# When the parts of the first layer's weight forms are made, and how the first maxima of W1 are taken

## The chip, the cores and the metric

The kernel runs on one core of a Trainium2 chip. A time is the device time of one execution in microseconds. It was measured three times: 1002.93, 1004.01 and 1005.3 us. The engines are TensorE (PE, with its weight loads as PEld), VectorE (DVE), ScalarE (ACT), GpSimd (POOL) and SyncE (SP), which issues the DMAs.

## What is computed

```python
def _attn_ref(q, k, v, tau):                      # q, k, v: (1, 6016, 256)
    qn = q / (np.linalg.norm(q, axis=1, keepdims=True) + 1e-06)
    kn = k / (np.linalg.norm(k, axis=1, keepdims=True) + 1e-06)
    s = kn.transpose(0, 2, 1) @ qn / tau
    a = np.exp(s - s.max(-1, keepdims=True))
    a /= a.sum(-1, keepdims=True) + 1e-09
    return v @ a                                  # (1, 6016, 256)

x = _attn_ref(q, k, v, tau).reshape(6016, 256)
h = x @ w_in1;  x = (h * np.cos(h)) @ w_out1      # 256 -> 2048 -> 256
h = x @ w_in2;  x = (h / (1 + np.exp(-h))) @ w_out2
```

The attention matrix a is only 256x256 (over channels), so the kernel folds it into the first layer: W1 = a @ w_in1.

## The kernel before, in words

Every matmul operand is kept in two parts, hi (the value rounded to the short form that the matmul takes) and lo (what is left), and a product takes three passes: hi by hi, lo by hi, hi by lo. The tokens are cut into 12 blocks, 11 of 512 and one of 384. The 2048 inner columns are cut into 8 pairs m of 256.

The program has these stages. The attention's scores and norms are made from q and k, about the first 50 us. Then W1 is folded in four pieces j (tile `wa0` to `wa3`, 512 columns each) while blocks 0 to 2 already run through the first layer in 24 units (`units`: a block b and a pair m). The rest of the first layer, and the second layer, run in slots after that. There a block's product is done in 7 products of quarter size instead of 8, on sums and differences of quarters: the forms. They need forms of the weights too: for each piece k of W1 `form_w1(k)` makes the four sums and differences, and `split_w1(k)` their hi and lo parts (`wf`).

There is no scheduler. `tc.manual_schedule()` leaves each engine's queue in the order in which the code emits the instructions, and an engine that waits holds up all that stands behind it. The order is set by tables: `BEFORE` lists the steps ahead of the first unit, `FORMING` says after which unit which steps of the forms stand, A0 for `form_w1(0)`, B0 for `split_w1(0)`, and V for a step of splitting and forming block 3's v (`v_steps`).

One pass of the loop over units, for unit i:
- PE: h of unit i (`emit_h`, 12 matmuls, L823), then, behind the other engines' steps in the code but alone on its own queue, o of unit i-2 (`emit_o1`, 12 matmuls, L851).
- ACT and DVE: the hi (L834) and lo (L838) of unit i-1, then the Sin of unit i (L1177) on ACT and the product with h (L1179) on DVE.
- At i = 4, 8, 12, 15 and 22 a small matmul of maxima (L442 or L477) and a comparison on DVE (L449 and L450, or L481 and L482) check that the arguments of Sin stay in range, and their room in PSUM is the one into which the next h goes.
- The steps of `FORMING[i]`. `form_w1` has two sums on DVE (L1031, `w1base`) and four sums or differences on POOL (L1039, `w1form`); `split_w1` has one copy on ACT (L1045, the hi) and two subtractions on POOL (L1047, the lo).
- The steps of x2, the input of layer 2 of a finished block (`begin_x2`: L917 to L919 on ACT, L936 to L945 on DVE or POOL).

A piece's base and form tiles have two buffers each (`raw` and `wv`), which v's form and the second layer's weights use too.

Ahead of the first unit, from `BEFORE`: `T0 T1` transposes, `rs` adds 1e-9 to the sums of the softmax and takes the reciprocal (L690, L691), `x0` takes v's maxima for block 0 (L430), `f00 f01` fold the two halves of piece 0 (PE L729, ACT L737), `l00 l01` make their lo (DVE L741), and `w00 w01` take the largest magnitude of piece 0 for each half of the channels (DVE L460), for the small matmul (L442) that stands between the h of unit 0 and of unit 1.

Of the kernel before, what the change touches and what calls it, by code (L numbers as in the profile page):

```python
# [9 lines left out]
F32 = mybir.dt.float32  # L10
F32R = mybir.dt.float32r
BF16 = mybir.dt.bfloat16
# [4 lines left out]
ALU = mybir.AluOpType  # L17
AX = mybir.AxisListType
PSUM = bass.MemoryType.PSUM

P = 128
C = 256
CH = C // P
# [35 lines left out]
THEN = ['', '', 'jO s0', '']  # L59
SIDE = [7, 11, 15, 20]  # L60
JOINED = 22
BEFORE = 'v0 sO T0 T1 bW kW x0 rs f00 lv l00 f01 l01 w00 w01 tb'
TURNS = 16
OPENED = 13
FORMING = {13: 'A0', 14: 'B0 A1', 15: 'B1 A2', 16: 'B2 A3', 17: 'B3 V', 18: 'V', 19: 'V'}
DOUBLED = (17, 22)
EARLY = {
# [21 lines left out]
@with_exitstack  # L89
def attention_then_two_ffns(ctx: ExitStack, tc: tile.TileContext, qk, vT, tau, w_in1, w_out1, w_in2, w_out2, outT):  # L90

    nc = tc.nc

    dp = ctx.enter_context(tc.tile_pool(name="dp", bufs=1, space=bass.MemoryType.DRAM))
    fp = ctx.enter_context(tc.tile_pool(name="fp", bufs=1))  # L100
    within = fp.tile([1, 1], I32, name="within")
    ctx.enter_context(tc.manual_schedule())
    kept = [[dp.tile([P, 2, 2, PIECE], F32, name=f"{s}{i}_kept") for i in range(4)] for s in ("wa", "wo1_")]
    with ExitStack() as rooms:
        direct(rooms, tc, qk, vT, tau, w_in1, w_out1, w_in2, w_out2, outT, dp, kept, within)
    inside = nc.values_load(within[0:1, 0:1], min_val=0, max_val=1)
    with tc.If(inside == 0):
        with ExitStack() as rooms:
            general(rooms, tc, vT, w_in2, w_out2, outT, kept)
# [117 lines left out]
def direct(ctx, tc, qk, vT, tau, w_in1, w_out1, w_in2, w_out2, outT, dp, kept, within):  # L227
    nc = tc.nc

    wp = ctx.enter_context(tc.tile_pool(name="wp", bufs=1))  # L230
# [12 lines left out]
    wa = [wp.tile(QUAD, F32R, tag="quad", name=f"wa{i}", bufs=8) for i in range(4)]  # L243
# [12 lines left out]
    largest = wp.tile([P, 4, CH], BF16, name="largest")  # L256
# [153 lines left out]
    def load_v(b):  # L410
        t0, n = BLOCKS[b]
        raw = io.tile([P, CH, TB], F32, tag="vraw", name=f"vraw{b}", bufs=1)
        nc.sync.dma_start(out=raw[:, :, :n], in_=vT.rearrange("(a p) n -> p a n", p=P)[:, :, t0 : t0 + n])
        return raw

    def span_of(b, raw, a=None):
# [9 lines left out]
            apply_absolute_value=True,  # L426
        )

    def span_of_first(b, raw):
        nc.vector.tensor_reduce(  # L430
            out=firsts[:, :, b],
            in_=raw.rearrange("p a (j n) -> p a j n", n=P),
            axis=AX.X,
            op=ALU.max,
            apply_absolute_value=True,
        )
# [22 lines left out]
    def span_of_weights(j, a):  # L459
        nc.vector.tensor_reduce(  # L460
            out=largest[:, j, a : a + 1],
            in_=fold_to(j, a, 0).bitcast(F32),
            axis=AX.XY,
            op=ALU.max,
            apply_absolute_value=True,
        )
# [19 lines left out]
    def split_v(b, raw):  # L486
        n = BLOCKS[b][1]
        hi, lo = xparts[1, b] = [x_tile(s, b) for s in ("hi", "lo")]
        nc.scalar.activation(halves(hi[:, :, :n]), turns(raw[:, :, :n]), AF.Copy)

        def low(eng=nc.vector):
            eng.tensor_tensor(
                out=halves(lo[:, :, :n]), in0=turns(raw[:, :, :n]), in1=halves(hi[:, :, :n]).bitcast(F32), op=ALU.subtract
            )

        return low
# [24 lines left out]
    rs = pp.tile([P, CH], F32, name="rs")  # L521
# [11 lines left out]
    calls = {  # L533
        "V": lambda: raw_v.update({0: load_v(0)}),
        "s0": lambda: low_v.update({0: split_v(0, raw_v[0])}),
        "v0": lambda: low_v.pop(0)(nc.gpsimd),
        "x0": lambda: span_of_first(0, raw_v.pop(0)),
        "lv": lambda: raw_v.update({1: load_v(1)}),
        "x1": lambda: span_of_first(1, raw_v[1]),
        "s1": lambda: low_v.update({1: split_v(1, raw_v[1])}),  # L540
        "v1": lambda: low_v.pop(1)(),
# [15 lines left out]
    def steps_of(names):  # L557
        for name in names.split():
            calls[name]()
# [107 lines left out]
    for a in range(CH):  # L667
        nc.vector.scalar_tensor_tensor(
            out=E[:, a], in0=S[a], scalar=r[:, 1, a : a + 1], in1=rq, op0=ALU.mult, op1=ALU.mult
# [54 lines left out]
    def fold_half(m):  # L724
        fold_room(0, m)
        for a in range(CH):
            pws[0, a] = pws[0, a][:, : TB // 2]
            for d in range(CH):
                nc.tensor.matmul(  # L729
                    pws[0, a],  # L730
                    ET[:, d, a * P : (a + 1) * P],
                    w1[:, d, m * TB // 2 : (m + 1) * TB // 2],
                    start=(d == 0),
                    stop=(d == CH - 1),
                )
        for a in range(CH):
            nc.scalar.activation(fold_to(0, a, 0)[:, m], pws[0, a], AF.Copy, scale=rs[:, a : a + 1])  # L737

    def fold_low_half(m):
        for a in range(CH):  # L740
            nc.vector.scalar_tensor_tensor(  # L741
                out=fold_to(0, a, 1)[:, m],
                in0=pws[0, a],
                scalar=rs[:, a : a + 1],
                in1=fold_to(0, a, 0)[:, m].bitcast(F32),
                op0=ALU.mult,
                op1=ALU.subtract,
            )

    def fold_whole(j):  # L750
        fold_room(j, 0)
        for a in range(CH):
            fold(j, a)

    def fold_highs(j):
        for a in range(CH):
            fold_high(j, a)

    def fold_to(j, a, i):
        return wa[j][:, i].rearrange("p m (a f) -> p a m f", a=CH)[:, a]  # L760

    def fold_low(j, a):
        nc.vector.scalar_tensor_tensor(
            out=fold_to(j, a, 1),
            in0=pws[j, a].rearrange("p (m f) -> p m f", m=2),
            scalar=rs[:, a : a + 1],
            in1=fold_to(j, a, 0).bitcast(F32),
            op0=ALU.mult,
            op1=ALU.subtract,
        )  # L770

    for j in range(NF // 4):
        calls[f"f{j}"] = lambda j=j: fold_whole(j)
        calls[f"e{j}"] = lambda j=j: fold_highs(j)
        for a in range(CH):
            calls[f"f0{a}"] = lambda a=a: fold_half(a)
            calls[f"l{j}{a}"] = (lambda j=j, a=a: fold_low(j, a)) if j else (lambda a=a: fold_low_half(a))
            calls[f"w{j}{a}"] = lambda j=j, a=a: span_of_weights(j, a)
    steps_of(BEFORE)
    early.close()  # L780

# [275 lines left out]
    def w2_slot(name, m):  # L1057
        w = w2[name][m]
        return lambda i, k: w[:, i, k - NS + w.shape[2]]
# [126 lines left out]
    for i, u in enumerate(units):  # L1186
        b, m = u
# [46 lines left out]
        if i == TURNS - 1:  # L1234
            vraw = load_v(FIRST + 1)
        for what in FORMING.get(i, "").split():
            if what == "V":
# [299 lines left out]
    for j in range(len(slots) + LAG2):  # L1537
        u, p, q, o = [slots[j - d] if 0 <= j - d < len(slots) else None for d in (0, 1, 2, LAG2)]
        if j < J:
# [5 lines left out]
        u, p, q, o = [  # L1545
            None if v is not None and v[:2] == (2, PLAIN) else v for v in (u, p, q, o)
        ]
        first_p, first_q, first_o = [v if v is not None and v[0] == 1 else None for v in (p, q, o)]
        p, q, o = [None if w_ is not None else v for v, w_ in ((p, first_p), (q, first_q), (o, first_o))]
# [5 lines left out]
        if p is not None:  # L1555
            k = (j - 1) % 2
            w = w2_slot("wi2", p[2])
            x = xparts[p[:2]]
            y, x0, z = ys[k][:, 1], xz[k][:, 1], xz[k][:, 0]
# [124 lines left out]
```

## Time and profile before

| | |
|---|---|
| times of three runs | 1002.93, 1004.01, 1005.3 us |
| the profiled execution | 1004.25 us |
| its span, first to last instruction | 1002.5 us |
| mean granted clock of TensorE | 0.998 |
| PE busy | 983.4 us (98%), 7080 matmuls |
| DVE, ACT, POOL busy | 819.1, 785.1, 400.4 us |
| chain that ended last | PE 87%, POOL 3% |

The chain is followed back from the last instruction; the matmuls' ends are modelled, so a gap between two matmuls is read best from when they start. Busy shares are means over the whole program; a wait counts in the stage in which it stands.

### The profile page before, as it was taken

To read this page: it belongs to the slowest core of one execution; us is meant where nothing else is said; L and a number is where in the kernel's file an instruction comes from. 1 tells how busy PE (TensorE), PEld (TensorE's weight loads), DVE (VectorE), ACT (ScalarE), POOL (GpSimd) and SP (SyncE) were. 2 spreads that over 40 slices of the span, in tenths; PEclk is the share of its full clock that TensorE was granted. 3 is DMA by queue.
4 is the path that set the end of the run, shared out by engine and by line. 5 is a ranking of instruction groups with operands and counts; after the bars stand their busy time and mean duration, and the time that the engine had idled before them with its cause. 6 is when DMAs were issued, how large, how long until landed. Compare 5 with 4: busy or idle time off the path is not lost.

```text
span 1002.5 us, 18729 instructions
## 1 busy us (share of the span) xinstructions
PE 983.4 (98%) x7080; PEld 929.8 (93%) x7080; DVE 819.1 (82%) x1287; ACT 785.1 (78%) x1442; POOL 400.4 (40%) x378
## 2 busy tenths in 40 slices
PE   9999998999999999999999999999999999999998
PEld 7878876899999999999999999999999999999997
DVE  6787775978787888787875789999999999999972
ACT  6776645688888888888876887887888888888863
POOL 4453358538777687787473111111111111111100
PEclk9999999999999999999999999999999999999999
DMA  8931021914334334334479731121121121121101
GB/s 334 383 110 63 1 93 72 350 74 160 137 126 142 133 144 142 152 131 153 147 256 383 312 147 43 55 95 49 47 96 49 48 96 55 45 93 39 36 18 41
DMA packets 35012, 126.59 MB, mean 126 GB/s; under 512 B 3170, under 2 KB 4450, under 8 KB 30178
## 3 DMA queue, kind: packets, MB, share of 16 engines
q1 hardware_dynamic: 34770, 125.12, 33.7%
q8 instruction: 57, 0.93, 0.4%
q14 instruction: 41, 0.34, 0.1%
q10 hardware_dynamic: 144, 0.20, 0.1%
HBM read 73.01 MB, written 52.30 MB: 125 GB/s over the span
## 4 chain that ended last, share of the span: by engine, by line
PE 87%; POOL 3%; ACT 1%; DVE 1%; issue 1%; ACTq 0%; POOLq 0%; DVEq 0%
PE o L1065 20%; PE xz L1065 20%; PE o L1421 16%; PE ys L1065 15%; PE o L851 6%; PE h L823 3%; POOL w1form L1039 2%; PE o L1105 2%; PE pw L711 1%; POOL wf L1047 1%; PE xz L1094 1%; PE ys L1094 1%; PE ys L1376 1%; PE xz L1376 1%; PE bound L823 1%
## 5 line engine op out<-in xcount | busy, mean ns | idle before, releaser
L881 DVE TENSOR_TENSOR lo<-t,hi 128x768 fp32r<-128x768 f32 (+1 forms) x176 | 194.8, 1116 | 29.2 <-ACT hi L873 29.1
L868 POOL TENSOR_TENSOR t<-t 128x256 f32<-128x256 f32 x88 | 64.4, 732 | 356.8 <-DVE t L865 312.9
L873 ACT ACTIVATE hi<-t 128x768 fp32r<-128x768 f32 (+1 forms) x176 | 168.6, 958 | 26.8 <-PE o L1065 25.9
L1421 PE MATMUL o<-hi,wo 128*128 128x512 f32 x512 | 142.0, 380 | 0.0
L1065 PE MATMUL o<-hi,wo 128*128 128x256 f32 x770 | 134.7, 275 | 0.0
L1065 PEld LDWEIGHTS o<-hi,wo 128*128 128x128 f32 x770 | 117.1, 192 | 0.0
L1065 PE MATMUL o<-lo,wo 128*128 128x256 f32 x385 | 105.9, 275 | 0.0
L1421 PEld LDWEIGHTS o<-hi,wo 128*128 128x128 f32 x512 | 87.4, 190 | 6.8
L1475 DVE TENSOR_TENSOR xz<-xz,t 128x512 f32<-128x512 f32 x64 | 44.8, 700 | 42.0 <-ACT t L1469 41.1
L1421 PE MATMUL o<-lo,wo 128*128 128x512 f32 x256 | 76.1, 380 | 0.0
L1065 PE MATMUL ys<-xhi,wf 128*128 128x256 f32 x384 | 74.2, 275 | 0.3 <-ACT u L1512 0.3
L1065 PEld LDWEIGHTS ys<-xhi,wf 128*128 128x128 f32 x384 | 67.7, 190 | 7.3 <-ACT u L1512 0.5
L1065 PEld LDWEIGHTS o<-lo,wo 128*128 128x128 f32 x385 | 73.9, 192 | 0.0
L1065 PE MATMUL xz<-xhi,wa 128*128 128x256 f32 x384 | 71.8, 276 | 0.0
L1580 ACT ACTIVATE ys<-xz 128x256 f32<-128x256 f32 x88 | 32.4, 368 | 45.8 <-PE xz L1065 44.9
L851 PE MATMUL o<-hi,wo 128*128 128x512 f32 (+1 forms) x256 | 64.2, 373 | 3.6 <-ACT hi L834 3.6
L1065 PEld LDWEIGHTS xz<-xhi,wa 128*128 128x128 f32 x384 | 62.8, 191 | 3.4
L1065 PE MATMUL xz<-x2hi,wf 128*128 128x256 f32 x352 | 65.8, 275 | 0.0
L1065 PE MATMUL xz<-x2hi,wa 128*128 128x256 f32 x352 | 65.8, 275 | 0.0
L860 DVE TENSOR_TENSOR t<-t 128x512 f32<-128x512 f32 x88 | 60.3, 685 | 0.1
L1610 ACT ACTIVATE t<-t 128x512 f32<-128x512 f32 x88 | 55.6, 632 | 2.2 <-DVE t L1115 2.1
L1466 ACT ACTIVATE ys<-xz 128x256 f32<-128x256 f32 x64 | 23.6, 368 | 40.9 <-PE xz L1065 39.8
(277 smaller groups left out, 3156.4 us busy)
## 6 DMA issues: line engine op xcount, KB each, us to landing
qk<-qk_dram SPq DMA_DIRECT2D x22, 512.0 KB, 7.7
x2hi<-xshi SPq DMA_DIRECT2D x11, 896.0 KB, 4.9
x2lo<-xslo SPq DMA_DIRECT2D x11, 896.0 KB, 6.9
wi_dram<-stage SPq DMA_DIRECT2D x8, 1024.0 KB, 3.8
wo_dram<-stage SPq DMA_DIRECT2D x8, 1024.0 KB, 4.2
vraw<-vT_dram SPq DMA_DIRECT2D x11, 512.0 KB, 4.1
outT_dram<-q SPq DMA_DIRECT2D x22, 256.0 KB, 2.0
xshi<-t SPq DMA_DIRECT2D x10, 512.0 KB, 5.4
```

The lines of the kernel that those rows point to most:

```text
L823: nc.tensor.matmul(hp[:, s, :n], wa_at(i, a, 2 * m + s), columns(x[k][:, a, :n]), start=((i, k) == passes[0] and a == 0), stop=((i, k) == ...
L851: nc.tensor.matmul(o[:, e, :n], wo1_at(i, f)[:, e * P : (e + 1) * P], columns(parts[k][:, s, :n]), start=(f == 0 and (i, k) == PASSES[0]), ...
L860: eng.tensor_tensor(out=t[:, 4:6, :c], in0=t[:, 0:1, :c].to_broadcast([P, 2, c]), in1=t[:, 1:3, :c], op=ALU.subtract)
L868: eng.tensor_tensor(out=t[:, 7, :c], in0=t[:, 3, :c], in1=t[:, 6, :c], op=ALU.subtract)
L873: nc.scalar.activation(hi[:, sl, :c], t[:, 1:][:, sl, :c], AF.Copy)
L881: nc.vector.tensor_tensor(out=lo[:, sl, :c], in0=t[:, 1:][:, sl, :c], in1=hi[:, sl, :c].bitcast(F32), op=ALU.subtract)
L1065: nc.tensor.matmul(out, w(p, ka), columns(x[r][:, kb - 1]), start=(start and i == 0), stop=(stop and i == 2), skip_group_check=True,)
L1421: nc.tensor.matmul(o[:, e], wo1_at(i, f)[:, e * P : (e + 1) * P], columns(parts[k][:, s]), start=(f == 0 and (i, k) == PASSES[0]), stop=(f ...
L1466: nc.scalar.activation(y2, x2, AF.Copy)
L1475: nc.vector.tensor_tensor(out=xz[k], in0=xz[k], in1=sines[:, 1], op=ALU.mult)
L1580: nc.scalar.activation(y2, x2, AF.Copy)
L1610: nc.scalar.activation(t[:, 0:2], t[:, 0:2], AF.Silu)
```

## The change

`FORMING` is written anew, the order of `BEFORE` is changed, and the first piece's maxima are taken in another way.

```diff
-BEFORE = 'v0 sO T0 T1 bW kW x0 rs f00 lv l00 f01 l01 w00 w01 tb'
+BEFORE = 'v0 sO T0 T1 bW kW rs f00 x0 lv l00 w00 f01 l01 w01 tb'
-FORMING = {13: 'A0', 14: 'B0 A1', 15: 'B1 A2', 16: 'B2 A3', 17: 'B3 V', 18: 'V', 19: 'V'}
+FORMING = {13: 'A0', 14: 'A1', 15: 'B0', 16: 'B1', 17: 'V', 18: 'V A2', 19: 'V', 20: 'B2 A3', 22: 'B3'}
+    half = wp.tile([P, CH], BF16, name="half")
+
+    def span_of_half(m):
+        to = half if m else largest[:, 0]
+        nc.vector.tensor_reduce(
+            out=to,
+            in_=wa[0][:, 0, m].rearrange("p (a f) -> p a f", a=CH).bitcast(F32),
+            axis=AX.X,
+            op=ALU.max,
+            apply_absolute_value=True,
+        )
+        if m:
+            nc.vector.tensor_tensor(out=largest[:, 0], in0=largest[:, 0], in1=half, op=ALU.max)
...
-            calls[f"w{j}{a}"] = lambda j=j, a=a: span_of_weights(j, a)
+            calls[f"w{j}{a}"] = (lambda j=j, a=a: span_of_weights(j, a)) if j else (lambda a=a: span_of_half(a))
```

For piece 0 `w00` and `w01` now stand for the first and the second half of its columns, each reduced for both halves of the channels in one instruction, and the two results are joined by a maximum. Lines behind the added function are 14 higher in the new file.

ACT at units 14 to 17, before (`wf0` to `wf3` are the hi of the forms, `hi` that of a unit, `t` a Sin, `xhi` the hi of v, `y` and `spare` are x2's):

```order
L489 ACTIVATE xhi2_1031<-vraw2_953 128x1024
L1045 ACTIVATE wf0_965<-w1form0_995 128x2x512
L834 ACTIVATE hi0_497<-t0_495 128x1024
L1177 ACTIVATE t1_496<-h1_7_1059,half_pi_98,smalls_102 128x1024
L1045 ACTIVATE wf1_966<-w1form1_1040 128x2x512
L834 ACTIVATE hi1_498<-t1_496 128x1024
L1177 ACTIVATE t0_495<-bound15_1080,half_pi_98,smalls_102 128x1024
L1045 ACTIVATE wf2_967<-w1form2_1093 128x2x512
```

The same place on ACT in the changed kernel:

```order
L503 ACTIVATE xhi2_1033<-vraw2_955 128x1024
L848 ACTIVATE hi0_499<-t0_497 128x1024
L1191 ACTIVATE t1_498<-h1_7_1058,half_pi_98,smalls_102 128x1024
L1059 ACTIVATE wf0_967<-w1form0_997 128x2x512
L848 ACTIVATE hi1_500<-t1_498 128x1024
L1191 ACTIVATE t0_497<-bound15_1079,half_pi_98,smalls_102 128x1024
L1059 ACTIVATE wf1_968<-w1form1_1039 128x2x512
```

The hi of unit 14 now stands ahead of `wf0`, and each `wf` of the first two pieces one unit later; `wf2` and `wf3` stand further down, behind the Sins of units 20 and 22.

POOL behind the forms of piece 0, before (`w1form` the forms, `wf` their lo):

```order
L1047 TENSOR_TENSOR wf0_965<-w1form0_995,wf0_965 128x512 x2
L1039 TENSOR_TENSOR w1form1_1040<-w1base1_1039 128x2x128 x2
L1039 TENSOR_TENSOR w1form1_1040<-w1form1_1040,w1base1_1039 128x2x128
L1039 TENSOR_TENSOR w1form1_1040<-w1base1_1039,w1form1_1040 128x2x128
L1047 TENSOR_TENSOR wf1_966<-w1form1_1040,wf1_966 128x512 x2
L1039 TENSOR_TENSOR w1form2_1093<-w1base2_1092 128x2x128 x2
L1039 TENSOR_TENSOR w1form2_1093<-w1form2_1093,w1base2_1092 128x2x128
L1039 TENSOR_TENSOR w1form2_1093<-w1base2_1092,w1form2_1093 128x2x128
```

The same place on POOL in the changed kernel (`vform` and `xlo` are the forms and the lo of v's block 3):

```order
L1053 TENSOR_TENSOR w1form1_1039<-w1base1_1038 128x2x128 x2
L1053 TENSOR_TENSOR w1form1_1039<-w1form1_1039,w1base1_1038 128x2x128
L1053 TENSOR_TENSOR w1form1_1039<-w1base1_1038,w1form1_1039 128x2x128
L1061 TENSOR_TENSOR wf0_967<-w1form0_997,wf0_967 128x512 x2
L1061 TENSOR_TENSOR wf1_968<-w1form1_1039,wf1_968 128x512 x2
L1012 TENSOR_TENSOR vform3_1155<-vraw3_1086 128x256 x2
L1012 TENSOR_TENSOR vform3_1155<-vraw3_1086,vform3_1155 128x256 x2
L1012 TENSOR_TENSOR xlo3_1153<-vraw3_1086,xhi3_1152 128x768
L1053 TENSOR_TENSOR w1form2_1196<-w1base2_1195 128x2x128 x2
```

The forms of piece 1 stand directly behind those of piece 0, both pieces' lo behind them, and v's forms and raw lo ahead of the forms of piece 2.

DVE ahead of the first unit, before (`rs` are the softmax's sums, `firsts` v's maxima, `largest` W1's):

```order
L680 COPY ET_125<-pt1_452 128x2x128
L430 TENSOR_REDUCE firsts_103<-vraw0_401 128x2x4
L690 TENSOR_SCALAR rs_127<-rs_127 128x2
L691 RECIPROCAL rs_127<-rs_127 128x2
L741 SCALAR_TENSOR_TENSOR wa0_89<-pw00_468,rs_127,wa0_89 128x256 x2
L741 SCALAR_TENSOR_TENSOR wa0_89<-pw01_479,rs_127,wa0_89 128x256 x2
L460 TENSOR_REDUCE largest_99<-wa0_89 128x1 x2
L449 TENSOR_REDUCE o1_0_514<-o1_0_514 128x1
```

The same place on DVE in the changed kernel:

```order
L694 COPY ET_126<-pt1_453 128x2x128
L704 TENSOR_SCALAR rs_128<-rs_128 128x2
L705 RECIPROCAL rs_128<-rs_128 128x2
L444 TENSOR_REDUCE firsts_103<-vraw0_402 128x2x4
L755 SCALAR_TENSOR_TENSOR wa0_89<-pw00_468,rs_128,wa0_89 128x256 x2
L433 TENSOR_REDUCE largest_99<-wa0_89 128x2
L755 SCALAR_TENSOR_TENSOR wa0_89<-pw01_481,rs_128,wa0_89 128x256 x2
L433 TENSOR_REDUCE half_104<-wa0_89 128x2
L441 TENSOR_TENSOR largest_99<-largest_99,half_104 128x2
L463 TENSOR_REDUCE o1_0_516<-o1_0_516 128x1
```

The reciprocal stands ahead of v's maxima, one reduction of W1 stands between the two lo steps, and one reduction and the maximum behind them.

## Rows read from the trace of the kernel before

**Rows 1.** Stages: us, then each engine's busy us, granted clock, DMA share, GB/s.

```profile
120.00:200.00 80.00, 72.58 (x326) 60.38 (x325) 59.04 (x59) 42.82 (x48) 50.25 (x37) 0.98 0.41 159
420.00:1002.00 582.00, 576.97 (x4750) 569.20 (x4749) 490.86 (x799) 465.34 (x938) 145.04 (x166) 1.00 0.29 107
```

**Rows 2.** Timeline of PE, 148 to 177 us: start, us, line, instruction, idle before.

```profile
148.37 1.99 PE L823 MATMUL bound<-xhi,wa 128*128 128x512 f32 x4 [2.42 <-DVE smalls L482]
...
155.31 1.03 PE L823 MATMUL h<-xhi,wa 128*128 128x512 f32 x4
...
160.49 1.03 PE L823 MATMUL h<-xhi,wa 128*128 128x512 f32 x4
...
164.55 1.13 PE L851 MATMUL o<-hi,wo 128*128 128x512 f32 x4 [1.31 <-ACT hi L834]
...
168.06 1.03 PE L823 MATMUL h<-xhi,wa 128*128 128x512 f32 x4
...
173.12 1.13 PE L851 MATMUL o<-hi,wo 128*128 128x512 f32 x4 [2.31 <-ACT hi L834]
...
176.91 1.03 PE L823 MATMUL h<-xhi,wa 128*128 128x512 f32 x4
```

**Rows 3.** One microsecond of the same view as rows 1, from 149 us.

```profile
149.00:150.00 1.00, 1.00 (x4) 0.82 (x3) 1.00 (x2) 0.00 (x0) 1.00 (x3) 0.50 0.97 410
```

**Rows 4.** Timeline of ACT, units 14 to 16.

```profile
145.42 1.04 ACT L834 ACTIVATE hi<-t 128x1024 fp32r<-128x1024 f32 x1
146.37 1.19 ACT L1177 ACTIVATE t<-h,half_pi,smalls 128x1024 f32<-128x1024 f32 x1
...
161.46 1.06 ACT L1045 ACTIVATE wf<-w1form 128x1024 fp32r<-128x1024 f32 x1 [5.50 <-POOL w1form L1039]
...
163.43 1.06 ACT L834 ACTIVATE hi<-t 128x1024 fp32r<-128x1024 f32 x1
```

**Rows 5.** Timeline of DVE, units 13 to 15.

```profile
137.70 1.28 DVE L1031 TENSOR_TENSOR w1base<-wa 128x512 f32<-128x512 f32 x2
138.90 1.22 DVE L838 TENSOR_TENSOR lo<-t,hi 128x1024 fp32r<-128x1024 f32 x1
140.03 1.22 DVE L1179 TENSOR_TENSOR t<-h,t 128x1024 f32<-128x1024 f32 x1
...
142.65 2.32 DVE L1031 TENSOR_TENSOR w1base<-wa 128x512 f32<-128x512 f32 x2
146.49 1.45 DVE L838 TENSOR_TENSOR lo<-t,hi 128x1024 fp32r<-128x1024 f32 x1 [1.52 <-ACT hi L834]
...
148.06 0.16 DVE L482 TENSOR_SCALAR smalls<-bound 128x1 f32<-128x1 f32 x1
```

**Rows 6.** POOL busy in L1039 (four pieces' forms), 136 to 186 us.

```profile
136.00:186.00 50.00, 16.89 (x16) 0.97 0.37 147
```

**Rows 7.** The same of L1047 (four pieces' lo).

```profile
136.00:186.00 50.00, 11.99 (x8) 0.97 0.37 147
```

**Rows 8.** The same of L998 (block 3's v: forms, raw lo, formed lo).

```profile
136.00:186.00 50.00, 11.97 (x7) 0.97 0.37 147
```

**Rows 9.** Groups by line of POOL, 136 to 186 us: busy, mean ns, idle before.

```profile
L998 POOL TENSOR_TENSOR xlo<-vform,xhi 128x512 fp32r<-128x512 f32 x2 | 4.5, 2266 | 0.0
```

**Rows 10.** Timeline of POOL: block 4's v.

```profile
192.68 2.37 POOL L998 TENSOR_TENSOR vform<-vraw 128x256 f32<-128x256 f32 x2 [7.46 <-DMA vraw<-vT_dram]
```

**Rows 11.** Timeline ahead of and at the first units.

```profile
51.98 1.21 DVE L430 TENSOR_REDUCE firsts<-vraw 128x8 bf16<-128x1024 f32 x1
...
53.59 0.84 ACT L737 ACTIVATE wa<-pw,rs 128x256 fp32r<-128x256 f32 x2 [0.47 <-DVE rs L691]
...
56.76 1.27 DVE L460 TENSOR_REDUCE largest<-wa 128x1 bf16<-128x512 f32 x2
...
58.09 0.18 PE L442 MATMUL o<-firsts,largest 128*128 128x4 bf16 x1 [0.41 <-DVE largest L460]
...
70.02 3.70 PE L711 MATMUL pw<-w,ET 128*128 128x512 f32 x8 [0.45 <-POOL w L320]
```

## The prediction

> **What bounds the kernel now.** The matmul engine's share comes first, by stages: from 420 us on it is busy 576.97 of 582 us, and what is missing there is the end of the program; from 120 to 200 us it is busy only 72.58 of 80, at a mean granted clock of 0.98 [rows 1]. That is the stage of units 13 to 23, in which the parts of W1's forms are made, and the change is made there. The reader is to see that time can come from hardly anywhere else.
>
> Second, the matmul timeline of that stage, read by the starts of h, the first product of a unit. A unit is 24 matmuls (12 of h, 12 of o) and takes 5.18 us where nothing waits, as from 155.31 to 160.49; that is 0.216 each. The h of unit 16 starts at 148.37 after 2.42 us idle. From there to the next h pass 6.94 us, 1.76 too many; from unit 18's h (160.49) to unit 19's (168.06) 7.57, 2.39 too many; from there to unit 20's (176.91) 8.85, 3.67 too many [rows 2]. Together 10.24 us.
>
> No wait stands beside the 1.76. They are the clock: 0.50, the level of 1.2 GHz, in the microsecond from 149 [rows 3], and four matmuls took 1.99 us. The engine had stood for 2.42 us; after 2.31 us before 173.12 four of them took 1.13 [rows 2], so that time the clock stayed. The length of the wait alone does not tell the two apart.
>
> Third, why h and o wait. On ACT the high part of the forms (wf, L1045) stands ahead of the unit's own high part (hi, L834). Before the third wf ACT sat idle 5.50 us until POOL had the form; hi came behind it, at 163.43, and at 145.42 in unit 14 [rows 4]. DVE's lo of unit 14 begins at 146.49 after 1.52 idle, and L482, which releases the h of unit 16, at 148.06 [rows 5]. So POOL and ACT in turn pace four units: forms of 16.89 / 4 = 4.2 us a piece [rows 6] and lo parts of 11.99 / 4 = 3.0 [rows 7].
>
> **The change, part by part.** No instruction of PE or SP moves; DVE gets two more.
>
> *Unit 14 to 16.* The wf of piece 0 goes behind the Sin of unit 15, so hi of unit 14 waits only for DVE's product: 140.03 + 1.22 = 141.25 instead of 145.42. Its lo is now held by DVE itself, whose row of work ends with the base of piece 1 at 142.65 + 2.32 = 144.97 [rows 5]. From lo's start to the h of unit 16 it took 148.37 - 146.49 = 1.88, so h starts at 146.85: 1.52 won, 0.9 of wait left. I take the clock to stay up, since that wait is shorter than the 1.31 before 164.55, behind which the engine went on at 1.13 for four [rows 2]: 1.76 won. Bounds: 0, where the drop comes all the same, and 1.76.
>
> *Units 16 to 19.* Are the 2.39 and 3.67 us gone, once hi is free of wf? I follow each new place of a wait, at POOL's mean durations. POOL has the first forms at 145.42 - 1.06 = 144.4 [rows 4]. The h of unit 15 ends 2.9 before the o that ended at 148.37 - 2.42, at 143.1, and Sin takes 1.19; ACT asks for wf 0 at 144.3 and waits 0.1. The forms of piece 1 last from 145.0 to 149.2 on POOL; wf 1 comes behind the Sin of unit 16, at 150.6, and does not wait. What lies between wf and hi in that unit (three copies) let hi start 163.43 - 161.46 = 1.97 behind wf; so hi at 152.6, lo 1.45 behind its 1.06: 155.2. The o of unit 16 is due at 146.85 + 5.18 + 5.18 + 2.59 = 159.8: over 4 us to spare. POOL goes on with both lo parts to 155.2, then the forms and raw lo of v (11.97 less 4.5 for the formed lo [rows 8, 9]) to 162.7, the forms of piece 2 (its base ends near 164.5) to 168.7, the formed lo to 173.2, lo 2 to 176.2 and the forms of piece 3 to 180.4. ACT asks for v's form near 166, for piece 2 at 171.4 and for piece 3 at 181.8 (Sin of units 19, 20, 22): 3, 2.7 and 1.4 us after POOL has them. Where POOL is 2 us slower, hi of unit 22 is late by 0.6, against some 3 us of room in o. So all of 2.39 + 3.67 = 6.06 is won; the bound below is 2.39, where the longer stall comes back once.
>
> DVE's bases of pieces 2 and 3 move to units 18 and 20, behind those units' products. With 1.3 to 2.3 us [rows 5] they go into units of 5.18 in which product and lo take 2.4 to 2.9; unit 18 also holds an x2 part as large as lo's three quarters, and overruns by some 0.5, covered by the 3 us that its lo has until o. If that cover were gone the 0.5 would show in o.
>
> *Bases beside POOL.* A base of two instructions takes 1.28 us before POOL begins (137.70) and 2.32 beside its forms; lo takes 1.22 and, beside POOL's lo parts, 1.45 [rows 5]. Behind the change POOL hardly rests from 139 to 186, so the long durations stand in the sums above. The Trainium skill (SBUF — State Buffer, Who interferes with whom) is harsher: of a DVE instruction with two inputs in SBUF and a GpSimd one that reads there, whichever starts second is blocked until the first has finished. By that rule lo of unit 14 could stand through a whole form, about 1.06 us at the mean, where the trace lengthens it by 0.23; the sum would be smaller by some 0.8, and I go by the row.
>
> *The front.* DVE took v's maxima (1.21 us at 51.98) ahead of the reciprocal for which ACT's fold waited until 53.59; now the reciprocal is first. That alone moves nothing, because the second half's fold waits for matmuls. What counts stands behind it: two reductions at 56.76, 1.27 us together, release the matmul at 58.09. Now the first half is reduced while DVE was idle, only one reduction is left behind the second half, and a maximum over 128x2 follows. No row shows that one; L482, as small, takes 0.16 [rows 5]. Half of 1.27 less 0.16 and its issue is 0.4; between 0 and the 0.6 that h of unit 1 waits in all I take 0.35. It travels through Sin, v's split and the decode to the matmuls that waited for POOL until 70.02 [rows 11]. v's second load waits for the maxima that now end 0.5 later; I price that at nothing, or the 0.35 back.
>
> Sum: 1.52 + 1.76 + 6.06 + 0.35 = 9.69. The profiled execution took 1004.25 us (its span 1002.5), 0.24 above the median of the runs shown; 1004.25 - 9.69 = 994.6 us. What is won by 200 us reaches the end, since the matmul engine has no gap behind it to give it back in [rows 1].
>
> **The rivals.**
> *Unit 16 keeps its wait and the clock drops (0.14).* For it: the h of unit 16 still waits for DVE, and POOL now runs through. If base and lo take 1.5 us longer, nothing is won there. Against it: the long durations are in the sum already. Left are 6.06 + 0.35: 997.8 us. The Trainium skill (TensorE: Matmul & The Clock Gate, HAM oscillation) has waits take the array to half its clock and the work behind them run cold; here one wait of three did. By that rule with the short wait 1.76 come back: 996.4 us.
>
> *The wait moves on (0.07).* Pieces 2 and 3 now share POOL with v's forms, and the margin at unit 22 is 1.4 us. If ACT meets POOL late at unit 20 or 22 as it did at 16 and 17, 2.39 to 3.67 come back: 997.0 to 998.3 us.
>
> *Nothing comes of it (0.04).* POOL's row of work falls behind throughout and both waits return, with the clock: 6.06 + 1.76 back, 1002.4 us or above.
>
> *Slower (0.03).* POOL begins the next block's v form near 186, when the matmul engine is 2 to 3 us further on than before; there POOL had 7.46 us idle ahead of it [rows 10]. ACT's copy of such a form stands ahead of its own work in each of seven blocks. If POOL is late for that copy from then on, each block loses the lateness; from 9.69 / 7 = 1.4 us a block it is slower than before, and at 2.5 us it is 994.6 + 17.5 = 1012 us. Against it: the copy comes two slots behind the form.
>
> **How the numbers follow.** The forecast has 0.72, the rivals 0.14, 0.07, 0.04 and 0.03. Under 0.2%, 2 us, a measurement of this kernel can't be told from no change. Faster by more: 0.72 + 0.14 + 0.07 = 0.93; same 0.04; slower 0.03. Low end: the waits of 10.24 and 0.6 at the front all won, 993.4, and 0.9 for the scatter of the runs: 992.5. High end: the first two rivals, 998.3.
>
> **What would show it.** Right: from 120 to 200 us the matmul engine's idle time falls from 7.4 us to near 1, and the clock stays 1.00; wf waits under 0.5 us on ACT; the o of units 16 and 17 waits for nothing; the h of unit 16 waits about 0.9 us, behind a base on DVE; the second matmul on the maxima comes at about 57.7 and the fold of piece 1 at 69.7. Wrong: an ACT wait above 3 us on wf of pieces 2 or 3 or on v's form, or a clock of 0.50 anywhere behind 60 us.

## The result, and the profile after

The changed kernel took 994.42 us (median of six runs, 993.16 to 996.48), the kernel before 1004.22 (six runs, 1002.93 to 1005.3). The ratio is 0.9905, with an interval of 0.9892 to 0.9917: 9.8 us less, where the prediction's sum had 9.69. The profiled execution took 994.43 us, its span 992.6 (before 1002.5), its mean granted clock was 0.999 (0.998). One execution of the second experiment below took 1456.11 us at a mean granted clock of 0.654, a slower state, and is left out of that experiment's median.

The stage of units 13 to 23 is where it went. The same windows as in [rows 1], the last one to the end of the shorter span, and the microsecond of [rows 3]:

```profile
120.00:200.00 80.00, 79.85 (x394) 68.90 (x393) 65.53 (x71) 51.11 (x63) 53.17 (x38) 1.00 0.47 178
420.00:992.00 572.00, 566.94 (x4683) 559.82 (x4681) 482.67 (x785) 455.86 (x920) 138.22 (x160) 1.00 0.29 106
149.00:150.00 1.00, 1.00 (x6) 0.89 (x5) 0.56 (x1) 0.98 (x1) 1.00 (x1) 1.00 0.99 418
```

From 120 to 200 us the matmul engine idles 0.15 us instead of 7.42, and the clock stays at 1.00. From 200 to 420 us it is busy 220.00 of 220 us in both traces, and from 420 us to the end it idles 5.06 us, before 5.03: nothing is given back.

The timeline of the matmul engine in that stage (start, us, line, instruction, idle before), against [rows 2]; line numbers are 14 higher than before:

```profile
146.09 1.10 PE L837 MATMUL bound<-xhi,wa 128*128 128x512 f32 x4 [0.15 <-DVE smalls L496]
...
151.35 1.03 PE L837 MATMUL h<-xhi,wa 128*128 128x512 f32 x4
...
156.53 1.03 PE L837 MATMUL h<-xhi,wa 128*128 128x512 f32 x4
...
161.71 1.03 PE L837 MATMUL h<-xhi,wa 128*128 128x512 f32 x4
...
164.30 1.03 PE L865 MATMUL o<-hi,wo 128*128 128x512 f32 x4
165.16 0.59 PE L865 MATMUL o<-lo,wo 128*128 128x512 f32 x2
...
166.89 1.03 PE L837 MATMUL h<-xhi,wa 128*128 128x512 f32 x4
```

These are the h of units 16 to 20, and between the last two the o of unit 17. The h of unit 16 starts 2.28 us earlier than before (146.09 against 148.37); the fold of piece 1 starts at 70.02 in both traces, so the starts can be compared as they stand. From there to unit 17's h pass 5.26 us where it was 6.94, 1.68 won. From unit 17's h to unit 20's pass 15.54, three units at the full pace; before it was 176.91 - 155.31 = 21.60, so 6.06 are won. Sum: 10.02, and unit 20 starts 176.91 - 166.89 = 10.02 earlier. No wait stands beside the o of unit 17, at 164.30 and 165.16; before, it waited 2.31 us and then 0.82.

ACT in units 13 to 20, against [rows 4]:

```profile
141.37 1.06 ACT L848 ACTIVATE hi<-t 128x1024 fp32r<-128x1024 f32 x1 [0.59 <-DVE widest L483]
...
146.29 1.07 ACT L1059 ACTIVATE wf<-w1form 128x1024 fp32r<-128x1024 f32 x1 [1.79 <-POOL w1form L1053]
...
150.18 1.07 ACT L1059 ACTIVATE wf<-w1form 128x1024 fp32r<-128x1024 f32 x1
...
165.66 1.04 ACT L1030 ACTIVATE xhi<-vform 128x1024 fp32r<-128x1024 f32 x1
...
170.84 1.04 ACT L1059 ACTIVATE wf<-w1form 128x1024 fp32r<-128x1024 f32 x1
```

The hi of unit 14 starts at 141.37 instead of 145.42. Only the first wf waits for POOL, 1.79 us, and behind it nothing is late: hi of unit 15 has until its o at 153.94.

DVE in units 13 to 15 against [rows 5], and POOL's form of piece 0 that ran beside it:

```profile
142.70 1.29 DVE L1045 TENSOR_TENSOR w1base<-wa 128x512 f32<-128x512 f32 x2
143.89 1.78 DVE L852 TENSOR_TENSOR lo<-t,hi 128x1024 fp32r<-128x1024 f32 x1
...
145.79 0.16 DVE L496 TENSOR_SCALAR smalls<-bound 128x1 f32<-128x1 f32 x1
```

```profile
141.50 3.09 POOL L1053 TENSOR_TENSOR w1form<-w1form,w1base 128x256 f32<-128x256 f32 x1
```

The base of piece 1 took 1.29 us, not 2.32. POOL was the slower for it: this form of 128x256 took 3.09, where the sixteen form instructions, in their three groups, had medians of 0.90, 1.05 and 1.59. It does not always go this way: in the last experiment, which is the same kernel, the base took 2.33 and this form 1.85.

The front, against [rows 11]:

```profile
50.91 3.62 PE L743 MATMUL pw<-w,ET 128*128 128x256 f32 x16
...
57.97 0.20 PE L456 MATMUL o<-firsts,largest 128*128 128x4 bf16 x2 [0.85 <-DVE largest L441]
58.04 1.11 PE L837 MATMUL h<-xhi,wa 128*128 128x512 f32 x4
...
70.02 2.41 PE L725 MATMUL pw<-w,ET 128*128 128x512 f32 x5 [0.57 <-POOL w L320]
```

```profile
50.28 2.42 POOL L506 TENSOR_TENSOR xlo<-vraw,xhi 128x1024 fp32r<-128x1024 f32 x1
...
51.46 1.27 DVE L704 TENSOR_SCALAR rs<-rs 128x2 f32<-128x2 f32 x1
...
52.76 0.17 DVE L705 RECIPROCAL rs<-rs 128x2 f32<-128x2 f32 x1
...
56.23 0.68 DVE L433 TENSOR_REDUCE half<-wa 128x2 bf16<-128x512 f32 x1
...
56.87 3.62 POOL L303 TENSOR_SCALAR w<-w 128x1024 f32<-128x1024 f32 x1
56.95 0.97 DVE L441 TENSOR_TENSOR largest<-largest,half 128x2 bf16<-128x2 bf16 x1
```

The times of the program's start scatter from run to run: the first matmul of the fold (L743) began at 51.44 before, at 50.91 here, and between 49.59 and 50.91 in the experiments. So the front is read as intervals from that matmul. The h of unit 1 came 6.69 us behind it before and comes 7.13 behind it now; the fold of piece 1 18.58 before, 19.11 now. The front lost 0.4 to 0.5 us, where 0.35 was predicted to be won. The maximum over 128x2 took 0.97, not 0.16, and the addition of 1e-9, now first on DVE, 1.27.

### The profile page after: what moved, and what is told of

Read it like the earlier page. It is cut to its first block, busy times and chain, and to the rows that moved or that the text cites. A ratio compares the mean times of both kernels' runs of the same rounds, so it can differ in the third digit from the quotient of the medians.

```text
span 992.6 us, 18733 instructions
## 1 busy us (share of the span) xinstructions
PE 980.5 (99%) x7080; PEld 928.6 (94%) x7080; DVE 820.7 (83%) x1288; ACT 785.3 (79%) x1442; POOL 402.9 (41%) x378
## 4 chain that ended last, share of the span: by engine, by line
PE 90%; DVE 2%; ACT 1%; issue 1%; POOL 0%; ACTq 0%; DVEq 0%
PE o L1079 20%; PE xz L1079 20%; PE o L1435 16%; PE ys L1079 15%; PE o L865 7%; PE h L837 4%; PE o L1119 2%; PE pw L725 1%; PE bound L837 1%; PE xz L1108 1%; PE ys L1108 1%; PE ys L1390 1%; PE xz L1390 1%; DVE xlo L506 0%; DVE lo L852 0%
```

## The experiments

My theory behind the result: all of the gain is the order of the forms' parts, and the front costs half a microsecond, because two small DVE instructions meet POOL there. Rivals: the front has a part in the gain; a single step of `FORMING` would have done; the small maximum is slow by its shape.

**The forms' order alone** (on the kernel before):

```diff
-FORMING = {13: 'A0', 14: 'B0 A1', 15: 'B1 A2', 16: 'B2 A3', 17: 'B3 V', 18: 'V', 19: 'V'}
+FORMING = {13: 'A0', 14: 'A1', 15: 'B0', 16: 'B1', 17: 'V', 18: 'V A2', 19: 'V', 20: 'B2 A3', 22: 'B3'}
```

> The new FORMING alone, the front as before. Theory: the whole gain is FORMING's (10.0 us between the o of unit 14 and the h of unit 20) and the new front costs about 0.45 us, because two 2-element DVE instructions stand beside a running POOL instruction (the addition to rs 1.27 us, the maximum 0.97). Then this kernel takes 993.9 us, ratio 0.9897, and its fold of piece 1 starts 18.6 us after the first fold matmul, as before (19.1 in the changed kernel). Rival: the new front wins the 0.35 us of the prediction and its lateness in the one profile is chance; then this kernel takes 994.8 us and shows the 18.6 us all the same, while the front alone is faster.

It took 994.2 us (ratio 0.9901, 0.9884 to 0.9917): the whole gain, as far as times can tell. Whether the front adds or takes half a microsecond is read from the traces. The h of unit 1 came 6.69 behind the first fold matmul, as before. The timeline of its matmuls:

```profile
50.91 3.62 PE L729 MATMUL pw<-w,ET 128*128 128x256 f32 x16
...
57.60 1.11 PE L823 MATMUL h<-xhi,wa 128*128 128x512 f32 x4
...
146.06 1.10 PE L823 MATMUL bound<-xhi,wa 128*128 128x512 f32 x4 [0.65 <-DVE smalls L482]
```

**The front alone** (on the kernel before):

```diff
-BEFORE = 'v0 sO T0 T1 bW kW x0 rs f00 lv l00 f01 l01 w00 w01 tb'
+BEFORE = 'v0 sO T0 T1 bW kW rs f00 x0 lv l00 w00 f01 l01 w01 tb'
+    (and span_of_half for piece 0's maxima)
```

> The new BEFORE and the maxima by halves alone, FORMING as before. Theory: 0.45 us slower than before, 1004.7 us; the h of unit 1 starts 7.1 us after the first fold matmul (before 6.69) and the fold of piece 1 19.1 us after it (before 18.58); all waits of units 16 to 19 as before. Rival: 0.35 us faster, 1003.9 us, the h of unit 1 at 6.3 us and the fold at 18.2.

It took 1004.85 us (median of nine executions), ratio 1.0011 (1.0001 to 1.0021): no gain, and a trace of a loss. The interval from the first fold matmul to h of unit 1 was 7.13, as in the changed kernel. In the middle it showed something else:

```profile
147.85 1.10 PE L837 MATMUL bound<-xhi,wa 128*128 128x512 f32 x4 [2.55 <-DVE smalls L496]
...
164.08 2.08 PE L865 MATMUL o<-hi,wo 128*128 128x512 f32 x4 [3.04 <-ACT hi L848]
...
169.36 1.42 PE L837 MATMUL h<-xhi,wa 128*128 128x512 f32 x4
...
172.83 1.13 PE L865 MATMUL o<-hi,wo 128*128 128x512 f32 x4 [0.33 <-ACT hi L848]
...
176.44 1.03 PE L837 MATMUL h<-xhi,wa 128*128 128x512 f32 x4
```

```profile
168.00:170.00 2.00, 2.00 (x6) 1.56 (x5) 1.22 (x2) 0.99 (x2) 0.90 (x2) 0.50 0.00 0
```

Behind the wait of 2.55 us four matmuls took 1.10, the full pace. Behind the next one, 3.04, they took 2.08; the granted clock was 0.50 there. So the clock fell once, as in the kernel before, but at another place, and it was still at 0.50 from 168 to 170 us. The stage lost no more by it: the waits of the o of unit 17 were 0.33 and 0.64 us instead of 2.31 and 0.82, and from the wait at unit 16 to the h of unit 20 there were 2.55 + (176.44 - 147.85) - 4 x 5.18 = 10.42 us too many, where the kernel before has 10.24. Here the slow stretch was in part time that would have been waited anyway.

**The copy and the lo parts of piece 0 back to unit 14** (on the changed kernel):

```diff
-FORMING = {13: 'A0', 14: 'A1', 15: 'B0', 16: 'B1', ...
+FORMING = {13: 'A0', 14: 'B0 A1', 16: 'B1', ...
```

> The changed kernel with the parts of piece 0 put back to unit 14 (FORMING 14: 'B0 A1'), all else as changed. Theory: hi of unit 14 waits again behind wf of piece 0, the h of unit 16 starts about 2.3 us later (148.4 instead of 146.1), and the clock falls behind that wait as before: 994.4 + 2.3 + 1.7 = 998.4 us; the o of units 16 and 17 wait for nothing. Rival: the clock fell for another reason than this wait and stays at 1.00: 996.7 us.

It took 996.88 us (0.9935, 0.9919 to 0.9952). Its h of unit 16 and 17, and the microsecond behind the wait:

```profile
148.43 1.10 PE L837 MATMUL bound<-xhi,wa 128*128 128x512 f32 x4 [2.54 <-DVE smalls L496]
...
153.68 1.03 PE L837 MATMUL h<-xhi,wa 128*128 128x512 f32 x4
```

```profile
149.00:150.00 1.00, 1.00 (x6) 0.88 (x5) 0.41 (x1) 0.49 (x1) 1.00 (x3) 1.00 1.01 426
```

The wait of the h is back, through the same chain as in [rows 4, 5]: ACT stood 3.79 us for POOL's form, hi began at 145.48, DVE's lo at 146.55. The h starts 2.34 us later than in the changed kernel (148.43 against 146.09), the span is 2.4 us longer (995.0 against 992.6) and the median 996.88 - 994.42 = 2.46. The clock stayed in this trace: 5.25 us from h to h. My expectation that the clock falls whenever this wait comes was wrong, and three of the four executions, 996.5 to 996.91 us, are as the rival said (996.7). The fourth took 998.72 us at a mean granted clock of 0.997, near the theory's 998.4; it was not profiled, so where its clock fell is not known.

**Piece 2 and 3 back to units 16 to 18** (on the changed kernel):

```diff
-FORMING = {..., 16: 'B1', 17: 'V', 18: 'V A2', 19: 'V', 20: 'B2 A3', 22: 'B3'}
+FORMING = {..., 16: 'B1 A2', 17: 'B2 A3 V', 18: 'B3 V', 19: 'V'}
```

> The changed kernel with pieces 2 and 3 one to two units behind their forms as well, but not from unit 18 on: FORMING 16: 'B1 A2', 17: 'B2 A3 V', 18: 'B3 V', 19: 'V'. Theory: POOL ends the forms of piece 2 near 160.3 and ACT asks for them at 155.4, so hi of unit 17 comes 4 us later, inside its slack of some 5; the forms of piece 3 end near 168.7, hi of unit 18 near 169.8, its lo near 171.5, and the o of unit 18, due at 169.5, waits about 2 us in all: 996.4 us. Rival: moving the first two pieces is all that counts and the later ones have slack in any order: 994.4 us and no wait of o.

It took 997.44 us (0.9939, 0.9923 to 0.9956), 3.0 more than the changed kernel. The matmuls of the o of units 17 and 18, and ACT:

```profile
164.79 0.70 PE L865 MATMUL o<-lo,wo 128*128 128x512 f32 x2 [0.41 <-DVE lo L852]
...
170.57 1.13 PE L865 MATMUL o<-hi,wo 128*128 128x512 f32 x4 [1.20 <-ACT hi L848]
...
171.92 0.70 PE L865 MATMUL o<-lo,wo 128*128 128x512 f32 x2 [0.21 <-DVE lo L852]
```

```profile
159.12 1.06 ACT L1059 ACTIVATE wf<-w1form 128x1024 fp32r<-128x1024 f32 x1 [4.67 <-POOL w1form L1053]
...
167.57 1.06 ACT L1059 ACTIVATE wf<-w1form 128x1024 fp32r<-128x1024 f32 x1 [3.49 <-POOL w1form L1053]
```

ACT stands 4.67 and 3.49 us for POOL's forms with hi behind it, and the o of units 17 and 18 are late. The wait of unit 18 is where it was expected; the 0.41 of unit 17 was expected to vanish in its slack. In the trace the two units lose 0.68 and 1.95 us, 2.6 in all, where 2 were expected. So with the waits behind the Sin, but pieces 2 and 3 not moved far, 3.4 of the 6.06 us stay won; the later units of pieces 2 and 3 are needed for the other 2.6.

**The maximum with one input** (on the changed kernel; both halves' maxima go to one tile, and a reduction over it replaces the maximum of two tiles):

```diff
-    half = wp.tile([P, CH], BF16, name="half")
+    by_half = wp.tile([P, CH, 2], BF16, name="by_half")
...
-            nc.vector.tensor_tensor(out=largest[:, 0], in0=largest[:, 0], in1=half, op=ALU.max)
+            nc.vector.tensor_reduce(out=largest[:, 0], in_=by_half, axis=AX.X, op=ALU.max)
```

> The changed kernel; the maximum of the two halves is a reduction over one small tile (one input in SBUF) in place of a two-input maximum. Theory: the maximum took 0.97 us because a DVE instruction with two inputs in SBUF stands for POOL's clamp, which runs there; a reduction has one input and takes 0.16 to 0.2 us as others of its size do. The h of unit 1 starts 6.35 us after the first fold matmul (changed kernel 7.13, before 6.69) and the fold of piece 1 18.3 after it (19.11, 18.58): 0.8 us faster than the changed kernel, 993.6 us. Rival: a small DVE instruction right behind the reductions that feed it takes its time in any form; then it takes about 1 us again and nothing moves, 994.4 us.

```profile
56.52 3.62 POOL L303 TENSOR_SCALAR w<-w 128x1024 f32<-128x1024 f32 x1
56.66 0.16 DVE L440 TENSOR_REDUCE largest<-by_half 128x2 bf16<-128x4 bf16 x1
...
58.04 1.22 DVE L443 TENSOR_REDUCE firsts<-vraw 128x8 bf16<-128x1024 f32 x1 [0.57 <-DMA vraw<-vT_dram]
```

The step takes 0.16 instead of 0.97, beside the same 3.62 us of POOL. The interval to h of unit 1 falls from 7.13 to 6.32, that to the fold of piece 1 from 19.11 to 18.33: v's maxima for the next block now wait 0.57 for a load. Time: 993.85 us (0.9897, 0.9882 to 0.9912), where the changed kernel beside it took 993.77 (last experiment): the 0.8 us stand in the trace, and the times do not show them.

**The same, with v's maxima first again** (on the one before):

```diff
-BEFORE = 'v0 sO T0 T1 bW kW rs f00 x0 lv l00 w00 f01 l01 w01 tb'
+BEFORE = 'v0 sO T0 T1 bW kW x0 rs f00 lv l00 w00 f01 l01 w01 tb'
```

> As the run before, and v's maxima ahead of the addition to rs again (BEFORE with 'x0 rs f00 lv l00 w00 f01 l01 w01'). Theory: moving rs ahead won nothing, since its addition stood 1.27 us for POOL's lo of v and the first fold's copy on ACT began at the same 2.13 us behind the first matmul; so the addition takes 0.16 again, the copy begins at the same time, v's second load is issued 0.4 us earlier, and the time is that of the run before, 993.6 us, 0.3 us less than FORMING alone. Rival: moving rs had its use and is lost here, the first copy starts 0.3 us later: 993.9 us or more.

The front on DVE and on ACT:

```profile
50.49 1.21 DVE L443 TENSOR_REDUCE firsts<-vraw 128x8 bf16<-128x1024 f32 x1
51.62 0.16 DVE L703 TENSOR_SCALAR rs<-rs 128x2 f32<-128x2 f32 x1
51.81 0.17 DVE L704 RECIPROCAL rs<-rs 128x2 f32<-128x2 f32 x1
```

```profile
52.09 0.84 ACT L750 ACTIVATE wa<-pw,rs 128x256 fp32r<-128x256 f32 x2 [0.47 <-DVE rs L704]
```

The addition takes 0.16 again, and ACT's first copy comes 2.14 us behind the first fold matmul; in the changed kernel, with rs first, it was 53.04 - 50.91 = 2.13. The early rs wins nothing, since its addition then takes 1.27. The load's wait is gone and the fold of piece 1 comes at 18.20. Time: 993.06 us (0.9896, 0.9882 to 0.991), the lowest median of all, 0.7 below the changed kernel beside it; times with this scatter do not tell the two apart, only the trace does (0.8 at h of unit 1, 0.9 at the fold).

**POOL kept quiet** (on the changed kernel; the clamp of the next part of the first layer's weight, L303, is not on POOL ahead of the first unit but on DVE in unit 1, and POOL's rounding, L298, stays; one execution):

```diff
-BEFORE = 'v0 sO T0 T1 bW kW rs f00 ...
+BEFORE = 'v0 sO T0 T1 bW rs f00 ...
-    'inner': {1: 'zW', ...
+    'inner': {1: 'cW', ...
```

> The changed kernel without POOL's clamp of W1's second word ahead of the first unit (DVE does it in unit 1 instead, 0.68 us there), the two-input maximum as changed. Theory: with POOL idle behind its rounding, the two-input maximum takes 0.16 to 0.2 us instead of 0.97 and the h of unit 1 starts 6.35 us after the first fold matmul. Rival: the maximum is slow by itself: 0.97 us again, 7.13. The time of the whole is not the question (within 1 us of the changed kernel).

```profile
55.91 0.16 DVE L441 TENSOR_TENSOR largest<-largest,half 128x2 bf16<-128x2 bf16 x1
```

The same maximum of two tiles takes 0.16 when POOL has nothing, and the h of unit 1 comes at 6.32: it is POOL beside it, not the shape. It took 993.9 us. DVE's clamp in unit 1 (0.68 us) stands ahead of the steps for which POOL and the fold of piece 1 wait, and most of what the maximum saves is lost there: that fold comes at 18.93.

**The changed kernel again**, on the chip of the last three:

> The changed kernel unchanged, beside the others on one chip. Theory and rival alike: 994.4 us; the h of unit 16 waits under 0.7 us, the o of units 16 and 17 not at all. Theory of the clock: where the drop comes varies from execution to execution among kernels with long waits, and this kernel has none behind 60 us, so the clock of the stage from 120 to 200 us is 1.00 again. Rival: it drops in it in some executions all the same.

```profile
50.77 1.28 DVE L704 TENSOR_SCALAR rs<-rs 128x2 f32<-128x2 f32 x1
...
56.26 0.99 DVE L441 TENSOR_TENSOR largest<-largest,half 128x2 bf16<-128x2 bf16 x1
```

993.77 us (0.9897, 0.9882 to 0.9912). The 1.28, the 0.99 and the intervals (7.15 and 19.03) come back: they are no scatter. The clock from 120 to 200 us is 1.00 in its trace, and the o of units 16 and 17 wait for nothing. Unit 16 does not come back as it was:

```profile
141.95 2.33 DVE L1045 TENSOR_TENSOR w1base<-wa 128x512 f32<-128x512 f32 x2
144.20 1.21 DVE L852 TENSOR_TENSOR lo<-t,hi 128x1024 fp32r<-128x1024 f32 x1
```

```profile
145.83 1.10 PE L837 MATMUL bound<-xhi,wa 128*128 128x512 f32 x4 [0.65 <-DVE smalls L496]
```

Here the base took its long time and lo its short one, the first wf waited for nothing, and the h of unit 16 waited 0.65 us. Seven of the traces have the changed order at units 13 to 15: the h of unit 16 waited 0.65 to 0.68 in five of them, and 0.15 and 0.16 in the other two, the trace of the result and that of the sixth experiment. None of the edits was made to choose between the two, and what decides is open.

## Why the prediction came out right, point by point

*Unit 16's wait: 1.52 predicted, 2.28 measured in the trace of the result, 1.78 in that of the repeat.* The chain was right (hi no longer behind wf, then DVE's base, lo, L496). In the trace of the result the base of piece 1, which I let end at 144.97 with 2.32 us, took 1.29, and lo began at 143.89. Of these 1.08 lo gave back 0.3 (1.78 where I had 1.45), which leaves the 0.76. In the repeat the base took 2.33, as predicted, and only lo was shorter (1.21); counted from the fold of piece 1, the h of unit 16 comes 145.83 - 69.26 = 76.57 us behind it, where it was 148.37 - 70.02 = 78.35. So the base was sized right for five traces of seven, and 0.5 of the 2.28 belongs to the one execution. The third experiment undoes this step alone, and the h starts 2.34 later.

*The clock: 1.76 predicted, 1.68 measured.* With a wait of 0.15 us, and of 0.65 in the repeat, the clock stayed at 1.00 in the stage. But the term is no fixed price of that wait. The clock fell behind a wait of 2.42 at unit 16 [rows 2, 3] and behind one of 3.04 at an o (second experiment), and did not behind 2.31 [rows 2], 2.55 and 2.54. What can be said is that the two traces with all of the waits (the kernel before, with 7.4 us of them, and the second experiment) each have one such stretch, and that the changed kernel has no long wait left there. That a short wait keeps the clock up is not shown for every execution: one of the six of the changed kernel had a mean granted clock of 0.996 and was the slowest, 996.48 us, while the other five had 0.999 to 1.000 and 993.16 to 995.3. It was not profiled. Why the clock falls at one place and not at the other stays open.

*Units 16 to 19: 6.06 predicted, 6.06 measured,* in the repeat too. The o waits of both units are gone whole. Within it two sizes were off. The wf of piece 0 was to wait 0.1 and waited 1.79 in the trace of the result, since POOL's two forms from 141.50 on ended 1.8 us later than before (none in the repeat). The base of piece 3 took 3.13, where 1.3 to 2.3 was allowed. The room behind both covered them.

*The front: +0.35 predicted, -0.4 to -0.5 measured.* This is the step that was wrong. It failed at "I take 0.35", from a maximum of 0.16 by the nearest row, L482, an instruction on 128x1 with one tensor as input. Beside POOL's clamp the maximum takes 0.97, and the half microsecond won by reducing the first half early is lost again. The signs named for it, 57.7 and 69.7, came at 57.97 and 70.02. The early reciprocal was to move nothing, and moves nothing; its addition, 1.27 instead of 0.16, holds back v's maxima and the load behind them, a term put at nothing: that load showed as 0.57 us of wait once the maximum was quick (fifth experiment). DVE got one instruction more (1288 against 1287), not two.

The sum: 10.02 in the stage less 0.5 at the front is 9.5, and the span shrank by 9.9; the program's start, 0.53 earlier in this trace, makes up the rest to 0.1. That the total of 9.69 was met to 0.1 is luck: a unit 16 that won 0.76 more than predicted stood against a front that came 0.8 worse, and the start of the program alone scatters by more than that (49.59 to 51.44 for the first fold matmul). By the repeat's trace the same sum is 1.78 + 1.68 + 6.06 - 0.45 = 9.07; its start was 1.21 earlier than before, and its span 10.3 shorter. What holds is the forecast for the order of the forms: 1.52 + 1.76 + 6.06 = 9.34 predicted, 10.02 and 9.52 in the two traces.

*The rivals.* None came true. POOL did not run late at unit 20 or 22, and v's form of the later blocks was not late for ACT: none of its seven later copies waited, and from 200 us on the matmul engine idles as before. The rival of the wait that moves on is what the fourth experiment shows, at units 17 and 18, when only half of the change is made.

## What to carry to other kernels

On queues that run strictly in order, look for the waiting instruction and for what is queued behind it: putting the waiter behind work that needs nothing of it, and giving what it waits for more time, won 6 us at two units here without one instruction less. Then spread what it waits for, or the wait returns one unit later. A small DVE instruction on the path that sets the end is to be priced by what POOL runs beside it and not by its size alone: the maximum of two inputs took 0.97 us here, and as a reduction with one input 0.16. And one trace of the changed kernel is not enough to settle a term of half a microsecond; the repeat moved unit 16 by that much.

## What the runs showed of the hardware that was not expected

A maximum over 128x2 took 0.97 to 0.99 us beside a 3.62 us POOL instruction and 0.16 without it; as a reduction of 128x4 it took 0.16 beside the same instruction. An addition of a constant on 128x2 took 1.27: POOL's lo of v had begun at 50.28 and taken 2.42, and the two ended at 52.73 and 52.70. The Trainium skill (SBUF — State Buffer, Who interferes with whom) says that reductions never contend with GpSimd on this chip, that tensor_scalar can and that a two-input instruction does, and that whichever comes second is blocked until the first has finished. The reductions and the addition agree. The maximum agrees only in part: it ended at 57.92, and POOL's instruction (56.87 + 3.62) ran to 60.49. What ended its block stays open.

The same pair can be charged to either engine, in the same program: DVE's base took 1.29 us and POOL's form beside it 3.09 in one execution of the changed kernel, and 2.33 and 1.85 in another. In the traces of the other experiments with this order it was 1.26 and 3.09 once, and 2.33 to 2.35 and 1.83 to 1.85 four times.

The clock's fall came behind waits of 2.42 and 3.04 us and not behind 2.31, 2.54 and 2.55, in kernels whose work around them differs by little. Where it came at unit 16 it cost 1.7 to 1.8 us; where it came at an o with waits behind it, those waits were shorter by 2.2 us, and the stage lost no more than before.
